# An attention and FFN kernel on one core: the softmax subtracts a row maximum taken by VectorE, and work moves between VectorE, ScalarE and GpSimd

## The chip, the core and the metric

One of the eight cores of a Trainium2 chip runs the whole kernel. The metric is the time of one execution on the device in microseconds (us). Five engines work side by side, each through its own instructions in order: TensorE (PE, matmuls; its weight loads are shown as PEld), VectorE (DVE), ScalarE (ACT), GpSimd (POOL) and SyncE (SP), which here only issues DMAs. They wait for each other through semaphores. PE writes its results to PSUM, eight banks of 128 partitions x 512 fp32 values.

## The reference, cut to what matters

x is 2048 x 448. After a layer norm it goes into an attention (16 query heads of 256, 8 key and value heads, the last 512 positions of the cache) and into a gated FFN; the result is x plus their product.

```
xn = layernorm(x)
q  = xn @ wq                                  # 16 heads of 256
k, v = the last 512 positions of the caches, each for two query heads
p  = softmax(q k^T * 256**-0.5)               # rows of 512
s  = (p v) @ wo
g  = silu((gelu(xn @ w_gate) * (xn @ w_up)) @ w_down)
out = x + s * g
```

Everything is bf16 with fp32 accumulation. A softmax whose rows are shifted by a constant gives the same p, so the kernel before takes the exponentials of the scaled scores as they are, with no maximum subtracted.

## The kernel before

The 2048 rows are cut into four chunks of 512, and each chunk into four tiles of 128. A small recorder (`R.op`) takes each operation with what it reads and writes, derives the semaphore waits from that, and keeps each engine's operations in the order in which the program names them. So the order of the Python loops is the order in each engine's queue.

**Head.** While the first tiles of x are loaded and normalized, PE runs a few warm-up matmuls and folds the last value head with its rows of wo: `fold_tr` (L384) transposes the last head of V into bank 0, `fold_copy` (L393) copies both halves to SBUF in one ACT instruction, `fold` (L397) multiplies them with the last rows of wo ("wo7", loaded by SP between the tiles of x, L301 to L309). The result vw stands in for V and wo of head 15 of every chunk.

**FFN.** For each chunk, 14 pairs of gate and up blocks (`two_blocks`, L464, two matmuls at a time on the two halves of PE's rows), gelu on ACT, product on DVE, then the down projection (`down`, L493). The down projection of the last chunk is spread as filler over the first 21 slots of the attention.

**Attention.** 64 heads follow one another (16 per chunk, index i), each with four tiles t of 128 queries. I call one pass of the inner loop a **slot**; slot n = 4i + t, 256 in all. In a slot (L685 to L703) PE does:

- `scores(i, t)` (L545): two matmuls into bank 4 + n % 2. ACT takes the exponential from PSUM into a bf16 tile `pr` and accumulates the row sum (L556); DVE takes the reciprocal (L558) and multiplies the tile by it (L559); SP transposes it by DMA into `pT` (L562).
- in even slots from slot 12 on, `values` (L564): four matmuls of a head three heads back, into bank 0, 1 or 6 by a list (L570); DVE copies the result to `oT` (L581), ACT for the last two heads.
- in odd slots from head 7 on, half an output projection (`outproj`, L588) of four heads into bank 7; when a tile's second half is done, DVE adds it to `acc` (L627). In the later chunks head 2 has one more in place of the values and head 6 has none (L691 to L701).
- at t = 0 of every eighth head (i = 7, 15, ..., 55), right after that slot's scores and values, the **query burst** (`q_burst`, L516): the queries of the next eight heads, in eight parts. Each part takes a pair of banks, (0,1), (2,3), (4,5) in turn, and is emptied by one ACT copy of 128x1024 (L527); each part's second phase is issued behind the next part's first. The eighth part has banks 2 and 3. A burst of four heads stands in slot 12; its second part has banks 4 and 5.

POOL loads weights during the FFN, and in the attention does SiLU (L646, L648) and the last products (L631, L633), each for one tile of 128 x 448. The score tiles `pr` rotate through 11 buffers.

The order inside a score tile's chain is set by these lines:

```
act(lambda e: e.activation(pr[s][:, :], bank(b), ACT.Exp, scale=scale, accum_out=den[:, s:s + 1]),
    r=[("ps", b)], w=[("pr%d" % s,), ("den", s)])
dve(lambda e: e.reciprocal(rden[:, s:s + 1], den[:, s:s + 1]), r=[("den", s)], w=[("rden", s)])
```

Of the kernel before, what the change touches and what calls it, by code (L numbers as in the profile page):

```python
# [5 lines left out]
ACT = mybir.ActivationFunctionType  # L6
ALU = mybir.AluOpType
BF16 = mybir.dt.bfloat16
F32 = mybir.dt.float32

LN_EPS = 1e-5
P = 128
# [132 lines left out]
def bass_recurrent_scan__sliding_block_cached__geglu_ffn__prompt_kernel(nc, A_x, A_k, A_v, A_wq, A_wo, B_x, B_wg, B_wu, B_wd, out):  # L145
    _, S, D = A_x.shape
    Hkv, Sk, Dh = A_k.shape[1], A_k.shape[2], A_k.shape[3]
    HD = A_wq.shape[1]
    Hq = HD // Dh
    W = min(4096, max(256, Sk // 4))  # L150
    F = B_wg.shape[1]
    QC, TPC, HP, KF = 512, 4, 64, 3
    NQC = S // QC
    NT = NQC * TPC
    NF, NJ, NE = F // P, W // P, Dh // P
    NO = Hq * NE
    assert S % QC == 0 and D == KF * P + HP and NE == 2 and NJ == 4 and Hq == 2 * Hkv and Hq % 4 == 0 and NF % 2 == 0
    scale = float(Dh) ** -0.5
# [3 lines left out]
    with es:  # L162
        off = [16512]

        def sb(name, shape, dt, at=None):
            n = 4 if dt == F32 else 2
            for x in shape[1:]:
                n *= x
            if at is None:
                at = off[0]  # L170
                off[0] += (n + 31) // 32 * 32
            return R.place(name, shape, dt, at), at + (n + 31) // 32 * 32

        ident, _ = sb("ident", [P, P], BF16)
        small, _ = sb("small", [P, 4], F32)
        stats, _ = sb("stats", [P, NT, 6], F32)
        mv, _ = sb("mv", [P, NT, 2], F32)
        std, _ = sb("std", [P, NT], F32)
        rstd, _ = sb("rstd", [P, NT], F32)
        den, _ = sb("den", [P, 16], F32)  # L180
        rden, _ = sb("rden", [P, 16], F32)

        xnT, _ = sb("xnT", [P, NQC, KF + 1, QC], BF16)
        gy, _ = sb("gy", [P, NT, D], BF16)
        kT, _ = sb("kT", [P, Hkv, NE, W], BF16)
        V, _ = sb("V", [P, NJ, Hkv, Dh], BF16)

        wq, _ = sb("wq", [P, KF, Hq, Dh], BF16)
        wq6, _ = sb("wq6", [P, Hq // 2, Dh], BF16)
        wo, _ = sb("wo", [P, Hq * NE, D], BF16)  # L190

        vw, _ = sb("vw", [P, NJ, D], BF16)
# [43 lines left out]
        def bank(b, n=512):  # L236
            return psum[:, b * 512:b * 512 + n]
# [26 lines left out]
        def load_x0(a, b):  # L264
            dma("sync", x4[:, a:b, :], x_view[:, 0, a:b, :], w=[("x4", t) for t in range(a, b)])
# [11 lines left out]
        def load_gu(s):  # L277
            load_w(0, s)
            load_w(1, s)
# [18 lines left out]
        def load_wo7():  # L298
            dma("sync", wo[:, NO - NE:NO, :], wo_v[:, NO - NE:NO, :], w=[("wo", "f")])
# [1 line left out]
        for t in range(2):  # L301
            load_x0(t, t + 1)
        load_v7()
        for t in range(2, TPC):
            load_x0(t, t + 1)
        load_wo7()
        load_gu(0)
        load_gu(1)
        load_gu6(5, NF, "sync")  # L309
# [72 lines left out]
        vT_keys = [("actT", NF - 3), ("actT", NF - 2)]  # L382

        def fold_tr():  # L384
            def run(e):
                for m in range(NE):
                    for j in range(NJ):
                        ins = e.transpose(bank(0).bitcast(BF16)[:, m * W + j * P:m * W + (j + 1) * P],  # L388
                                          V[:, j, Hkv - 1, m * P:(m + 1) * P], ident[:, :])
                return ins  # L390
            pe(run, r=[("V", "f"), ("ident",)], w=[("ps", 0)])

        def fold_copy():  # L393
            act(lambda e: e.activation(vT.rearrange("p m k -> p (m k)"), bank(0).bitcast(BF16), ACT.Copy),  # L394
                r=[("ps", 0)], w=vT_keys)

        def fold(j):  # L397
            def run(e):
# [117 lines left out]
        def q_burst(i0, heads):  # L516

            c, h0 = divmod(i0, Hq)

            def part(n, ph):  # L520
                hp, e_ = divmod(n, 2)
                s, h = 2 * (n % 3 if heads == 8 else (0, 2, 1, 0)[n] if i0 else (n + 2) % 4), h0 + 2 * hp
                buf, name, _ = q_slot(i0 + 2 * hp)
                two_blocks(ph, c, s, [wq[:, :, h + m, e_ * P:(e_ + 1) * P] for m in range(2)],
                           wq6[:, h // 2, e_ * P:(e_ + 1) * P], wq_keys)
                if ph:
                    act(lambda e: e.activation(  # L527
                        buf[:, :, e_, :], psum[:, s * 512:(s + 2) * 512].rearrange("p (a q) -> p a q", a=2), ACT.Copy),
                        r=[("ps", s), ("ps", s + 1)], w=[(name, e_)])

            for n in range(heads + 1):
                if n < heads:
                    part(n, 0)
                if n:
                    part(n - 1, 1)
# [4 lines left out]
        def p_slot(i):  # L540

            n = (i - i // Hq) % NPT
            return (pTf, ("pT", "f")) if folded(i) else (pT[:, n, :, :], ("pT", n))

        def scores(i, t):  # L545
            g, n = (i % Hq) // 2, i * TPC + t
            b, s = 4 + n % 2, n % NPR
            buf, name, a = q_slot(i)

            def run(e):  # L550
                for k in range(NE):
                    ins = e.matmul(bank(b), lhsT=buf[:, a, k, t * P:(t + 1) * P], rhs=kT[:, g, k, :],  # L552
                                   start=k == 0, stop=k == NE - 1)
                return ins
            pe(run, r=[("kT", g), (name, 0), (name, 1)], w=[("ps", b)])
            act(lambda e: e.activation(pr[s][:, :], bank(b), ACT.Exp, scale=scale, accum_out=den[:, s:s + 1]),  # L556
                r=[("ps", b)], w=[("pr%d" % s,), ("den", s)])
            dve(lambda e: e.reciprocal(rden[:, s:s + 1], den[:, s:s + 1]), r=[("den", s)], w=[("rden", s)])  # L558
            dve(lambda e: e.tensor_scalar(pr[s][:, :], pr[s][:, :], rden[:, s:s + 1], None, op0=ALU.mult),  # L559
                r=[("pr%d" % s,), ("rden", s)], w=[("pr%d" % s,)])  # L560
            dst, key = p_slot(i)
            dmaT(dst[:, :, t * P:(t + 1) * P], pr[s][:, :], r=[("pr%d" % s,)], w=[(*key, t)], lane="p%d" % s)  # L562

        def values(i, e_):  # L564
            g = (i % Hq) // 2
            idx = (i % 4) * NE + e_
            src, pkey = p_slot(i)
            at = 2 * i + e_ + 6

            b = (0, 6, 0, 6, 0, 1, 6, 6)[at % 8] if at < 2 * NI else (0, 6, 1, 0, 6, 1)[at - 2 * NI]  # L570

            def run(e):
                for j in range(NJ):
                    ins = e.matmul(bank(b), lhsT=V[:, j, g, e_ * P:(e_ + 1) * P], rhs=src[:, j, :],  # L574
                                   start=j == 0, stop=j == NJ - 1)
                return ins
            pe(run, r=[(*pkey, t) for t in range(TPC)] + ([("V", j) for j in range(NJ)] if g < Hkv - 1 else [("V", "f")]),
               w=[("ps", b)])
            dst, key = oT[(i // 4) % 2][:, idx, :], ("oT%d" % ((i // 4) % 2), idx)
            if i < NI - 2:  # L580
                dve(lambda e: e.tensor_copy(dst, bank(b)), r=[("ps", b)], w=[key])  # L581
            else:
                act(lambda e: e.activation(dst, bank(b), ACT.Copy), r=[("ps", b)], w=[key])

        def n_pieces(G):
            return 3 * NE + NJ if folded(4 * G + 3) else 4 * NE
# [55 lines left out]
        def silu(n):  # L642

            s = n % 2
            act(lambda e: e.activation(tmp[:, s, :], gy[:, n, :], ACT.Tanh, scale=0.5), r=[("gy", n)], w=[("tmp", s)])  # L645
            pool(lambda e: e.tensor_scalar(tmp[:, s, :], tmp[:, s, :], 1.0, 0.5, op0=ALU.add, op1=ALU.mult),  # L646
                 r=[("tmp", s)], w=[("tmp", s)])
            pool(lambda e: e.tensor_tensor(gy[:, n, :], tmp[:, s, :], gy[:, n, :], ALU.mult),  # L648
                 r=[("tmp", s), ("gy", n)], w=[("gy", n)])
# [34 lines left out]
        outs = [(G, t) for G in range(NG) for t in range(TPC)]  # L684
        for i in range(NI):  # L685
            for t in range(TPC):
                scores(i, t)
                if 4 * i + t in fill:
                    down(NQC - 1, *fill[4 * i + t])

                early = i >= Hq and i % Hq == 2  # L691
                if t % 2 == 0 and early:
                    n = n_pieces(outs[1][0])
                    outproj(*outs[1], range(n * t // 4, n * (t + 2) // 4), b=6)
                elif t % 2 == 0 and 4 * i + t >= 12:
                    values(*pv.pop(0))
                if 7 <= i and t % 2 and not (i >= Hq and i % Hq == 6):
                    n = n_pieces(outs[0][0])
                    outproj(*outs[0], range(n * (t - 1) // 4, n * (t + 1) // 4))
                    if t == TPC - 1:  # L700
                        del outs[0:1 + early]  # L701
                if t == 0 and (i == 3 or i % 8 == 7) and i + 1 < NI:
                    q_burst(i + 1, 4 if i == 3 else 8)  # L703
            if i % Hq in (7, 9, 11, 13):
                silu(i // Hq * TPC + (i % Hq - 7) // 2)

        for what in "vvovovo":
            if what == "v":
# [38 lines left out]
```

## Time and profile before

| | us |
|---|---|
| median of 3 runs (lowest, highest) | 558.71 (557.78, 558.84) |
| the profiled execution | 558.57 |
| its span, first to last instruction | 556.8 |
| mean granted TensorE clock | 1.00 |

The span is one profiled execution; what lies around it is 558.57 - 556.8 = 1.8 us. In the span, the head takes the first 10.4 us, the FFN of the four chunks ends at about 127.4 us, the first query burst (four heads) runs from there to 133.6, the slots of the attention run from 133.6 to about 539, and DVE's last product ends at 554.8.

How to read the lines of the profile: L552 is a line of the kernel; then the engine, the operation, output <- input by the program's names (`ps` is PSUM), partitions x elements and type. A line of the timeline begins with the start and the duration in us and ends, in brackets, with the idle time before it and what ended that. Lines with xN are N instructions of one kind with little between them, taken together. SPq rows are DMA issues, with no bracket. ACT's exponential has a second row, ACTIVATION_READ_ACCUMULATOR, which writes out the row sum.

### The profile page before, as it was taken

The numbers are of one execution on the slowest core, as the hardware profiler recorded it, in microseconds if no ns is written. First come the engines' busy times: TensorE is split into PE (matmuls) and PEld (weight loads), VectorE is DVE, ScalarE is ACT, GpSimd is POOL, SyncE is SP. The second block draws the span as 40 slices with busy tenths as digits, with TensorE's granted clock in tenths as the row PEclk, the third lists the DMA queues.
The fourth block names the chain that finished last, engine by engine and source line by source line (L and its number), as shares of the span: only waits on it lengthen the run. The fifth ranks groups of instructions, "written<-read, shape, count | busy, mean of one in ns | idle before, by whom it ended". The sixth has DMA issues, their size and how long they took to land.

```text
span 556.8 us, 9924 instructions
## 1 busy us (share of the span) xinstructions
PE 552.5 (99%) x3550; PEld 261.4 (47%) x3550; DVE 313.7 (56%) x822; ACT 295.6 (53%) x688; POOL 88.4 (16%) x125
## 2 busy tenths in 40 slices
PE   8999999999999999999999999999999999999997
PEld 6444444444444444444444444444444444444445
DVE  5535436043463678077728744772688077628775
ACT  5333324237655665555575556556665655575640
POOL 0131213200000121002301110131121002311134
DMA  8863534952544354245544552547345254635452
GB/s 233 292 140 70 132 86 95 233 146 54 98 86 77 58 98 93 58 85 94 129 75 96 101 95 39 96 95 143 66 96 101 42 86 97 130 79 105 95 96 52
DMA packets 165440, 57.65 MB, mean 104 GB/s; under 512 B 155648, under 2 KB 162304, under 8 KB 165392
## 3 DMA queue, kind: packets, MB, share of 16 engines
q1 hardware_dynamic: 162048, 44.64, 41.5%
q0 software_dynamic: 3040, 12.16, 8.0%
q8 instruction: 28, 0.46, 0.4%
q10 hardware_dynamic: 304, 0.22, 0.1%
q14 instruction: 20, 0.16, 0.1%
HBM read 17.92 MB, written 1.84 MB: 35 GB/s over the span
## 4 chain that ended last, share of the span: by engine, by line
PE 98%; DMA 1%; ACT 0%; SPq 0%; DVE 0%; issue 0%
PE ps L472 33%; PE ps L552 20%; PE ps L574 19%; PE ps L604 18%; PE ps L496 8%; DMA V<-in_A_v_cache_dram 1%; PE ps L400 0%; PE ps L388 0%; ACT actT L394 0%; SPq L249 0%; ACT xnT L370 0%; PE ps L357 0%; ACT std L373 0%; DVE tmp L615 0%; DVE xr L617 0%
## 5 line engine op out<-in xcount | busy, mean ns | idle before, releaser
L556 ACT ACTIVATE pr<-ps 128x512 bf16<-128x512 f32 x256 | 152.5, 597 | 120.4 <-PE ps L552 119.1
L552 PE MATMUL ps<-kT,qT 128*128 128x512 bf16 x512 | 150.9, 380 | 0.0
L558 DVE RECIPROCAL rden<-den 128x1 f32<-128x1 f32 x256 | 41.4, 162 | 154.2 <-ACT pr L556 139.6
L574 PE MATMUL ps<-pT,V 128*128 128x512 bf16 x480 | 123.1, 379 | 0.0
L559 DVE TENSOR_SCALAR pr<-pr,rden 128x512 bf16<-128x512 bf16 x256 | 106.0, 414 | 9.0
L604 PE MATMUL ps<-wo,oT 128*128 128x448 bf16 (+1 forms) x498 | 111.0, 346 | 0.0
L472 PE MATMUL ps<-xnT,wq 64*128 64x512 bf16 x896 | 98.3, 377 | 0.0
L527 ACT ACTIVATE qT<-ps 128x1024 bf16<-128x1024 f32 x64 | 64.5, 1022 | 43.4 <-PE ps L472 43.1
L472 PE MATMUL ps<-xnT,wu 64*128 64x512 bf16 x336 | 82.4, 377 | 0.0
L472 PE MATMUL ps<-xnT,wg 64*128 64x512 bf16 x336 | 82.0, 377 | 0.0
L581 DVE CAST oT<-ps 128x512 bf16<-128x512 f32 x118 | 80.5, 683 | 0.7 <-PE ps L574 0.6
L490 DVE TENSOR_TENSOR actT<-ps,hb 128x512 bf16<-128x512 f32 x56 | 38.5, 692 | 65.9 <-ACT hb L489 61.7
L552 PEld LDWEIGHTS ps<-kT,qT 128*128 128x128 bf16 x512 | 49.2, 98 | 55.4 <-issue 4.0
L574 PEld LDWEIGHTS ps<-pT,V 128*128 128x128 bf16 x480 | 47.0, 98 | 56.3
L604 PEld LDWEIGHTS ps<-wo,oT 128*128 128x128 bf16 x498 | 48.4, 98 | 48.6 <-DVE acc L627 1.0
L472 PEld LDWEIGHTS ps<-xnT,wq 64*128 64x128 bf16 x896 | 43.1, 94 | 54.5 <-DVE rden L558 1.7
L489 ACT ACTIVATE hb<-ps 128x512 bf16<-128x512 f32 x56 | 33.1, 593 | 38.8 <-PE ps L472 38.6
L556 ACT ACTIVATION_READ_ACCUMULATOR pr<-ps 128x1 f32 x256 | 50.2, 196 | 0.0
L496 PE MATMUL ps<-wd,actT 128*128 128x448 bf16 x224 | 46.2, 353 | 0.0
L472 PEld LDWEIGHTS ps<-xnT,wg 64*128 64x128 bf16 x336 | 31.3, 94 | 20.5 <-issue 1.1
L472 PEld LDWEIGHTS ps<-xnT,wu 64*128 64x128 bf16 x336 | 31.3, 94 | 19.9
L646 POOL TENSOR_SCALAR tmp<-tmp 128x448 f32<-128x448 f32 x16 | 9.0, 563 | 197.9 <-ACT tmp L645 197.9
(60 smaller groups left out, 264.0 us busy)
## 6 DMA issues: line engine op xcount, KB each, us to landing
pT<-pr SPq DMA_TRANSPOSE x240, 2.5
wq<-in_A_wq_dram POOLq DMA_DIRECT2D x14, 256.0 KB, 3.6
wo<-in_A_wo_dram POOLq DMA_DIRECT2D x3, 896.0 KB, 9.0
V<-in_A_v_cache_dram POOLq DMA_DIRECT2D x4, 448.0 KB, 6.5
xr<-in_A_x_dram POOLq DMA_DIRECT2D x4, 448.0 KB, 4.2
wd<-in_B_w_down_dram SPq DMA_DIRECT2D x1, 1568.0 KB, 15.1
x<-in_A_x_dram SPq DMA_DIRECT2D x3, 448.0 KB, 9.3
out_dram<-xr POOLq DMA_DIRECT2D x3, 448.0 KB, 3.7
```

The lines of the kernel that those rows point to most:

```text
L472: ins = e.matmul(bank(s + m)[:, q0:q1], lhsT=lhsT, rhs=xnT[lo:lo + HP, c, k, q0:q1], start=ph == 0 and k == 0, stop=ph == 1 and k == KF - 1)
L489: act(lambda e: e.activation(hb[:, h, :], bank(s), ACT.Gelu_apprx_tanh), r=[("ps", s)], w=[("hb", h)])
L490: dve(lambda e: e.tensor_tensor(actT[:, f, :], bank(s + 1), hb[:, h, :], ALU.mult), r=[("ps", s + 1), ("hb", h)], w=[("actT", f)])
L496: pe(lambda e, f=f: e.matmul(bank(b, D), lhsT=actT[:, f, t * P:(t + 1) * P], rhs=wd[:, f, :], start=f == 0, stop=f == NF - 1), r=[("actT", ...
L527: act(lambda e: e.activation(buf[:, :, e_, :], psum[:, s * 512:(s + 2) * 512].rearrange("p (a q) -> p a q", a=2), ACT.Copy), r=[("ps", s), ...
L552: ins = e.matmul(bank(b), lhsT=buf[:, a, k, t * P:(t + 1) * P], rhs=kT[:, g, k, :], start=k == 0, stop=k == NE - 1)
L556: act(lambda e: e.activation(pr[s][:, :], bank(b), ACT.Exp, scale=scale, accum_out=den[:, s:s + 1]), r=[("ps", b)], w=[("pr%d" % s,), ("de ...
L558: dve(lambda e: e.reciprocal(rden[:, s:s + 1], den[:, s:s + 1]), r=[("den", s)], w=[("rden", s)])
L559: dve(lambda e: e.tensor_scalar(pr[s][:, :], pr[s][:, :], rden[:, s:s + 1], None, op0=ALU.mult), r=[("pr%d" % s,), ("rden", s)], w=[("pr%d ...
L574: ins = e.matmul(bank(b), lhsT=V[:, j, g, e_ * P:(e_ + 1) * P], rhs=src[:, j, :], start=j == 0, stop=j == NJ - 1)
L581: dve(lambda e: e.tensor_copy(dst, bank(b)), r=[("ps", b)], w=[key])
L604: ins = e.matmul(bank(b, D)[:, lo:hi], lhsT=lhsT, rhs=rhs, start=idx == 0, stop=idx == n8 - 1)
```

## The change

In words: the scale of the scores moves into the copy of the queries. DVE takes the negated maximum of each score row from PSUM into `nmax`, and the exponential gets it as its bias. Reciprocal, multiply and transposing DMA become a step of their own, `normalize`, which is issued two slots later (`LAG`); the multiply of tile t = 3 goes to POOL. Scores rotate over banks 4, 5, 2 for the first 24 slots and over banks 2 to 5 from then on. All copies of values to `oT` are done by ACT. In the head, wo7 is loaded ahead of x's fourth tile, and the fold's transposes and its copy are split over banks 0 and 1.

```
-        for t in range(2, TPC):
-            load_x0(t, t + 1)
+        load_x0(2, 3)
         load_wo7()
+        load_x0(3, 4)
...
         def fold_tr():
-            def run(e):
-                for m in range(NE):
-                    for j in range(NJ):
-                        ins = e.transpose(bank(0).bitcast(BF16)[:, m * W + j * P:m * W + (j + 1) * P],
-                                          V[:, j, Hkv - 1, m * P:(m + 1) * P], ident[:, :])
+            def run(e, m):
+                for j in range(NJ):
+                    ins = e.transpose(bank(m).bitcast(BF16)[:, j * P:(j + 1) * P], V[:, j, Hkv - 1, m * P:(m + 1) * P], ident[:, :])
                 return ins
-            pe(run, r=[("V", "f"), ("ident",)], w=[("ps", 0)])
+            for m in range(NE):
+                pe(lambda e, m=m: run(e, m), r=[("V", "f"), ("ident",)], w=[("ps", m)])
         def fold_copy():
-            act(lambda e: e.activation(vT.rearrange("p m k -> p (m k)"), bank(0).bitcast(BF16), ACT.Copy),
-                r=[("ps", 0)], w=vT_keys)
+            for m in range(NE):
+                act(lambda e, m=m: e.activation(vT[:, m, :], bank(m).bitcast(BF16)[:, 0:W], ACT.Copy),
+                    r=[("ps", m)], w=[vT_keys[m]])
...
-                        buf[:, :, e_, :], psum[:, s * 512:(s + 2) * 512].rearrange("p (a q) -> p a q", a=2), ACT.Copy),
+                        buf[:, :, e_, :], psum[:, s * 512:(s + 2) * 512].rearrange("p (a q) -> p a q", a=2), ACT.Copy, scale=scale),
...
+        LAG = 2
+        BY_POOL = (3,)
+
+        def s_bank(n):
+            return (4, 5, 2)[n % 3] if n < 6 * TPC else 2 + n % 4
+
         def scores(i, t):
             g, n = (i % Hq) // 2, i * TPC + t
-            b, s = 4 + n % 2, n % NPR
+            b, s = s_bank(n), n % NPR
...
-            act(lambda e: e.activation(pr[s][:, :], bank(b), ACT.Exp, scale=scale, accum_out=den[:, s:s + 1]),
-                r=[("ps", b)], w=[("pr%d" % s,), ("den", s)])
+            dve(lambda e: e.tensor_reduce(nmax[:, s:s + 1], bank(b), mybir.AxisListType.X, ALU.max, negate=True),
+                r=[("ps", b)], w=[("nmax", s)])
+            act(lambda e: e.activation(pr[s][:, :], bank(b), ACT.Exp, bias=nmax[:, s:s + 1], accum_out=den[:, s:s + 1]),
+                r=[("ps", b), ("nmax", s)], w=[("pr%d" % s,), ("den", s)])
+
+        def normalize(i, t):
+            s = (i * TPC + t) % NPR
             dve(lambda e: e.reciprocal(rden[:, s:s + 1], den[:, s:s + 1]), r=[("den", s)], w=[("rden", s)])
-            dve(lambda e: e.tensor_scalar(pr[s][:, :], pr[s][:, :], rden[:, s:s + 1], None, op0=ALU.mult),
-                r=[("pr%d" % s,), ("rden", s)], w=[("pr%d" % s,)])
+            if t in BY_POOL:
+                pool(lambda e: e.tensor_tensor(pr[s][:, :], pr[s][:, :], rden[:, s:s + 1].to_broadcast([P, W]), ALU.mult),
+                     r=[("pr%d" % s,), ("rden", s)], w=[("pr%d" % s,)])
+            else:
+                dve(lambda e: e.tensor_scalar(pr[s][:, :], pr[s][:, :], rden[:, s:s + 1], None, op0=ALU.mult),
+                    r=[("pr%d" % s,), ("rden", s)], w=[("pr%d" % s,)])
             dst, key = p_slot(i)
             dmaT(dst[:, :, t * P:(t + 1) * P], pr[s][:, :], r=[("pr%d" % s,)], w=[(*key, t)], lane="p%d" % s)
...
-            if i < NI - 2:
-                dve(lambda e: e.tensor_copy(dst, bank(b)), r=[("ps", b)], w=[key])
-            else:
-                act(lambda e: e.activation(dst, bank(b), ACT.Copy), r=[("ps", b)], w=[key])
+            act(lambda e: e.activation(dst, bank(b), ACT.Copy), r=[("ps", b)], w=[key])
...
             for t in range(TPC):
+                n = i * TPC + t
                 scores(i, t)
+                if n >= LAG:
+                    normalize(*divmod(n - LAG, TPC))
...
+        for n in range(NI * TPC - LAG, NI * TPC):
+            normalize(*divmod(n, TPC))
```

## The prediction

> **What bounds the kernel now.** First the page: busy time, then the chain that ended last.
>
> ```profile
> PE 552.5 (99%) x3550; PEld 261.4 (47%) x3550; DVE 313.7 (56%) x822; ACT 295.6 (53%) x688; POOL 88.4 (16%) x125
> ...
> PE 98%; DMA 1%; ACT 0%; SPq 0%; DVE 0%; issue 0%
> ```
>
> TensorE (PE) is the bound; nothing else holds 2% of the chain. In the list of waits PE's own come to 1.4 us, all before 10.39 us, where the matmul stream begins. The built order of instructions shows that the change leaves PE's sequence as it is, matmul for matmul. So nothing is to be had behind 10.39 us: there the change can only make PE wait. I therefore looked at what follows each PE write to a bank that now has a new reader. A slot is one score tile (128 queries of one head, 256 slots). The timeline around the query burst at slot 60:
>
> ```profile
> 219.07 0.60 PE L552 MATMUL ps<-kT,qT 128*128 128x512 bf16 x2
> ...
> 219.70 0.60 ACT L556 ACTIVATE pr<-ps 128x512 bf16<-128x512 f32 x1 [0.50 <-PE ps L552]
> ...
> 221.56 0.59 PE L552 MATMUL ps<-kT,qT 128*128 128x512 bf16 x2
> ...
> 221.99 1.03 PE L574 MATMUL ps<-pT,V 128*128 128x512 bf16 x4
> ...
> 222.94 12.26 PE L472 MATMUL ps<-xnT,wq 64*128 64x512 bf16 x112
> ...
> 233.09 1.02 ACT L527 ACTIVATE qT<-ps 128x1024 bf16<-128x1024 f32 x1 [0.49 <-PE ps L472]
> 234.60 1.94 ACT L527 ACTIVATE qT<-ps 128x1024 bf16<-128x1024 f32 x2 [0.49 <-PE ps L472]
> 235.14 0.61 PE L552 MATMUL ps<-kT,qT 128*128 128x512 bf16 x2
> 235.58 0.92 PE L604 MATMUL ps<-wo,oT 128*128 128x448 bf16 x4
> 236.34 0.60 PE L552 MATMUL ps<-kT,qT 128*128 128x512 bf16 x2
> ```
>
> Matmuls overlap, so I count from start to start: scores 0.43 us, values 0.86, half an output projection 0.76. An even slot is 1.30, an odd one 1.19, four are 4.98. A score is ready for its reader 0.63 after its start (219.07 to 219.70). The burst follows slot 60 directly, and the scores of slot 61 (235.14) follow the burst directly, while ScalarE's (ACT's) last two query copies run until 234.60 + 1.94 = 236.54. Before, slot 61 writes bank 5, freed long ago; the last copy reads banks 2 and 3.
>
> VectorE (DVE), three rows of its timeline beside GpSimd's (POOL's):
>
> ```profile
> 198.05 1.03 POOL L648 TENSOR_TENSOR gy<-tmp,gy 128x448 bf16<-128x448 f32 x1
> 198.07 0.16 DVE L558 RECIPROCAL rden<-den 128x1 f32<-128x1 f32 x1
> 198.27 0.96 DVE L559 TENSOR_SCALAR pr<-pr,rden 128x512 bf16<-128x512 bf16 x1
> ...
> 199.16 0.68 DVE L581 CAST oT<-ps 128x512 bf16<-128x512 f32 x1
> 199.76 0.15 DVE L558 RECIPROCAL rden<-den 128x1 f32<-128x1 f32 x1
> 199.94 0.35 DVE L559 TENSOR_SCALAR pr<-pr,rden 128x512 bf16<-128x512 bf16 x1
> ```
>
> A multiply (L559) takes 0.35 alone and 0.96 where POOL's tensor_tensor runs: it ends with POOL's, and the next DVE instruction starts 0.08 behind it. The reciprocal is not held. DVE's instructions overlap too: reciprocal to multiply 0.20, multiply to the next 0.27 (201.02 - 200.76 = 0.26 elsewhere), CAST to the next 0.60 for a duration of 0.68.
>
> **The change, step by step.**
>
> Row maximum: 256 reductions, 128x512 from PSUM; before has none. Nearest row, L581 (same shape read from PSUM): 0.68 long, 0.60 to the next. Bounds: 0.53 to the next (three of L409's 448 columns take 1.68, one 0.61) and 0.68. I take 0.60, and 0.68 until the exponential may start. The 118 CASTs go to ACT (0.60 each, L583), a quarter of the multiplies to POOL: L633's 1.03 for 448 columns, by width 1.18. Bounds 1.0 and, should the broadcast operand be slow, 2.1, twice L633's.
>
> Exponential: a bias by pointer. The square root with one takes 292 ns (L373), the same width without 203 (L291): +0.09, 0.69 in all; bounds 0.60 and 0.69. ACT then has, per four slots, 4 x (0.69 + 0.10) + 2 x 0.60 = 4.4 of 4.98: no bound by itself. The scale moved into the query copy costs nothing (an immediate either way).
>
> DVE per four slots: 4 maxima 2.40, 3 x (0.20 + 0.27) = 1.41, a reciprocal 0.10, one accumulation 0.55: 4.46 of 4.98. Each slot queues its maximum, then the reciprocal and multiply of the slot two before; the accumulation stands behind t=3. Followed in that order with t=0 at time 0: the t=0 maximum stands behind the accumulation of the slot before and starts at 1.06 instead of 0.63; maxima t=1, 2, 3 start at 2.13, 3.12, 4.42; POOL's multiply runs 2.97 to 4.15 and costs the one multiply behind it about 0.2. The next t=0 starts at 1.06 again: DVE just keeps up. With 0.68 for a maximum it is 1.14. So:
>
> 1. **Behind a burst.** Slot 61 now takes bank 2 + 61 % 4 = 3, which the last query copy reads: PE waits from 235.14 to 236.54, 1.40 us. Every 8-head burst ends so (behind slot 28 the last two copies start at 182.57 and run 1.94, and PE goes on at 183.11: again 1.40): 7 x 1.40 = **9.8**. Bounds 1.2 to 1.9 each.
> 2. **Into a burst.** The second part writes banks 2 and 3, 2.16 us after the burst slot starts; bank 2 holds that slot's scores. Maximum from 1.06, exponential from 1.79, done 2.48, seen 2.53: PE waits 0.37, say 0.4; 7 x 0.4 = **2.8**. Bounds 0 (DVE free at 0.63) and 1.0.
> 3. **Slots 4 to 12.** Here PE needs only 0.76 a slot (137.95 to 144.05 for eight), there are three banks, and DVE needs 1.07 with a multiply, 0.70 without, plus up to 0.6 per POOL multiply. Maximum 4 starts at 139.1 behind the down-projection's CAST; with 1.07, 0.70 and POOL's locks the ninth starts at 144.4, its exponential is done 1.47 later, 145.84, and only then may scores 12 (144.05 before) write that bank: 1.8 late. Maximum 12 starts at 148.05 behind another CAST, its exponential ends at 149.5, and the second part of the 4-head burst, which writes bank 4 too, would be there at 148.0: 1.5 more. **3.3**; bounds 2 and 5.
> 4. **Slots 21 to 28.** No projection yet, 0.87 a slot. Slot 24 takes bank 2 right after slot 23 (the new rule of banks): maximum 23 starts at 166.6, its exponential ends at 168.07, slot 24 was due at 166.07: 2.0. The burst behind slot 28 then waits 0.9 instead of the 0.4 of step 2: **2.5** in all; bounds 1 and 3.5.
> 5. **Heads 22, 38, 54** have no projection: four slots in 3.46 for a DVE that needs 4.2, and a burst follows: 3 x 0.8 = **2.4**; bounds 1 and 4.
> 6. **Two values in bank 6 running**, two slots apart. The copy is now on ACT behind the t=0 exponential and ends 0.2 too late; eight such pairs between bursts: **1.6**; bounds 0 and 4.
> 7. **POOL's other work** (16 SiLU pairs, 32 products) holds multiplies while DVE has little to spare: in the trace 28 of 256 multiplies take 0.75 or more. Bounds 0 and 8; I take **2**, nearer to the rows in which DVE has slack.
> 8. **Head.** The fold matmuls start at 7.78, when wo7 lands (issued 3.13, 4.5 to landing). Issued 0.5 earlier, they start when the warm-up matmuls end, 7.55: **-0.2**. The split copy ends 0.4 earlier, hidden by that DMA. x's fourth tile, 0.5 later, still makes its transpose at 9.34. Bounds -0.5 and +0.3.
>
> Hidden: SP has one transposing DMA per slot as before, in the same order, now behind POOL's multiply every fourth time; values use a tile 7 slots (8.7 us) after its normalization is issued, and multiply plus landing is 1.2 + 2.5. At the end PE has 14 us of work behind the last scores, so the lag of two shows nowhere.
>
> Sum: 9.8 + 2.8 + 3.3 + 2.5 + 2.4 + 1.6 + 2.0 - 0.2 = 24.2. The profiled execution took 558.57 (span 556.8), 0.14 under the median: 558.57 + 24.2 = **582.8**.
>
> **Rivals.**
>
> A. *DVE becomes the bound* between bursts, if its instructions don't overlap: 4 x 0.68 + 4 x 0.16 + 3 x 0.35 + 0.62 + a lock of 0.44 = 5.47 for 4.98. Over 56 heads 27 us, with steps 1 and 3 558.57 + 27.4 + 9.8 + 3.3 = 599. For it: DVE has under 0.5 us to spare per head. Against: the spacings above. The Trainium skill ("VectorE: DVE Perf Modes", The DRAIN you can't avoid) says the next instruction doesn't start until the pipe is empty, save where it isn't held; the 0.60 behind a 0.68 CAST is the exception, so the rule itself would give this rival, the rows do not.
>
> B. *Only the fixed wait remains*: DVE keeps up everywhere but in slots 4 to 12 (lower bound 2): 558.57 + 9.8 + 2 = 570.4. For it: DVE is 56% busy. Against: slots at 0.76 us.
>
> C. *PE's clock drops after the waits.* The first 32 matmuls of 128 columns take 3.60 us, 0.11 each; eight of the same later 0.62, at most 0.08: PE starts slow for some 3.6 us. If each burst's wait brought that back, 1.8 us lost each: 582.8 + 12.6 = 595. Against: the granted clock reads 1.00 everywhere, and 1.4 us is short. The Trainium skill ("TensorE: Matmul & The Clock Gate", A second HAM failure mode) reports a clock that swings from small idles between banks; no row here shows it.
>
> D. *Not slower*: the head's earlier start of 0.2 (at most 0.5) is all that is left, 558.3. It decides if the last query copy is out before slot 61 starts; it would have to end 1.40 earlier, with ACT free before it and PE's last part still to come. Faster by more than 0.5 has no place.
>
> **How the numbers follow.** Forecast (574 to 592) 0.62; A 0.15; B 0.14; C 0.05; D 0.04. The range takes in A, B and C: 570 to 600. About 0.2% (1.1 us) is what a measurement here can tell: slower 0.96, same 0.02, faster 0.02.
>
> **What will show it.** Step 1: seven waits of PE at the score line for ACT's query copy, 1.4 each. Steps 2 to 5: PE waits at the query line and at scores for ACT's exponential, near 138 to 170 us and ahead of the bursts. Step 6: values waiting for ACT's copy. The maximum's row: 0.68. POOL's multiply: 1.2. A is right if PE waits in every head; B if only step 1 is there. I am wrong in kind if PE has no wait at the score line behind a burst.

## The result, and the profile after

The changed kernel takes **584.37 us** (median of 4 runs, 583.20 to 584.89) against 558.78 before: the ratio is 1.0459, 95% interval 1.0446 to 1.0473. The forecast was 582.8. The profiled execution has a span of 583.1 us, 26.3 longer. Its page opens with the busy times; further down stand the groups of the new work (mean ns of one, then the idle time before them and its releaser):

```profile
PE 554.1 (95%) x3517; PEld 264.2 (45%) x3550; DVE 356.6 (61%) x896; ACT 375.2 (64%) x807; POOL 154.2 (26%) x189
...
L563 DVE TENSOR_REDUCE nmax<-ps 128x1 f32<-128x512 f32 x256 | 175.5, 686 | 138.6 <-PE ps L559 134.1
L565 ACT ACTIVATE pr<-ps,nmax 128x512 bf16<-128x512 f32 x256 | 175.9, 687 | 77.2 <-PE ps L590 29.8
...
L572 POOL TENSOR_TENSOR pr<-pr,rden 128x512 bf16<-128x512 bf16 x64 | 66.6, 1041 | 237.0 <-DVE rden L570 233.2
...
L575 DVE TENSOR_SCALAR pr<-pr,rden 128x512 bf16<-128x512 bf16 x192 | 75.8, 395 | 6.8
```

PE's busy time grew by 1.6 us, its span by 26.3: PE waits. (Of PE's 3550 matmuls 33 have no record in this trace; all weight loads have.) Neither DVE nor ACT comes near its limit on the whole. The page's chain breaks off after a tenth of the span, as it does in some traces with all records, so PE's own waits are the view to read (total us, times, longest):

```profile
PE ps L559 <- ACT qT L528: 11.3, 7, 1.6
PE ps L473 <- ACT pr L565: 4.7, 8, 1.1
PE ps L559 <- ACT pr L565: 2.9, 4, 2.0
PE ps L590 <- ACT oT L596: 2.2, 7, 0.6
PE ps L590 <- DMA pT<-pr: 1.6, 1, 1.6
```

The first line is the wait behind the bursts: scores (L559) for the query copy (L528), seven times. Its 11.3 us is too high, because all seven times the first matmul behind the wait is one without a record. The second is the wait into the bursts (L473 for the exponential), the third slots 4 to 12 and slot 24, the fourth the values in bank 6. The fifth was not forecast. The burst of slot 60, in the changed kernel's timeline:

```profile
230.79 0.59 PE L559 MATMUL ps<-kT,qT 128*128 128x512 bf16 x2
...
231.22 1.03 PE L590 MATMUL ps<-pT,V 128*128 128x512 bf16 x4
231.30 0.62 DVE L640 TENSOR_TENSOR acc<-ps,acc 128x448 f32<-128x448 f32 x1
...
231.83 0.68 DVE L563 TENSOR_REDUCE nmax<-ps 128x1 f32<-128x512 f32 x1
232.18 1.04 PE L473 MATMUL ps<-xnT,wq 64*128 64x512 bf16 x8
...
232.60 0.69 ACT L565 ACTIVATE pr<-ps,nmax 128x512 bf16<-128x512 f32 x1 [0.81 <-PE ps L590]
...
233.18 0.19 ACT L565 ACTIVATION_READ_ACCUMULATOR pr<-ps,nmax 128x1 f32 x1
...
233.52 11.40 PE L473 MATMUL ps<-xnT,wq 64*128 64x512 bf16 x104 [0.30 <-ACT pr L565]
...
244.31 1.94 ACT L528 ACTIVATE qT<-ps 128x1024 bf16<-128x1024 f32 x2 [0.49 <-PE ps L473]
246.30 0.11 PEld L559 LDWEIGHTS ps<-kT,qT 128*128 128x128 bf16 x2 [1.88 <-ACT qT L528]
246.53 0.38 PE L559 MATMUL ps<-kT,qT 128*128 128x512 bf16 x1 [1.61 <-ACT qT L528]
```

The maximum of slot 60 starts 1.04 us after its scores (forecast 1.06), behind the accumulation at 231.30. The burst's second part waits for that slot's bank. Behind the burst the weight loads of the scores start 0.05 after the last copy's end, 246.25. The row at 246.53 is the second of the two matmuls (x1 where there should be x2).

Because PE's instructions are the same in both kernels, the start of each weight load can be set against the same one in before. The difference grows where PE waits or its clock falls, and only there. That gives the whole loss by place:

| place | forecast, us | in the trace |
|---|---|---|
| 1 behind seven bursts | 9.8 | 10.2 (7 x 1.46) |
| 2 into seven bursts | 2.8 | 3.3 (7 x 0.47) |
| 3 slots 4 to 12 | 3.3 | 3.1 |
| 4 slot 24 and the burst behind it | 2.5 | 2.5 |
| 5 heads without projection | 2.4 | 1.2 (3 x 0.40) |
| 6 values in bank 6 | 1.6 | 2.8 (8 pairs) |
| 7 GpSimd's other work | 2.0 | no place of its own |
| 8 head | -0.2 | -0.2 |
| PE's clock behind slot 24 | rival C | 1.7 |
| last values | 0 | 1.8 |
| sum (from unrounded terms) | 24.2 | 26.3 |

Step 8's -0.2 can't be told from chance. The start of the matmul stream differs by more than that from run to run: over the eleven traces with the changed head it lies from 0.69 us earlier to 0.83 us later than in the one trace of before, and in two of the variants below that keep before's head 0.16 earlier and 0.14 later.

### The profile page after: what moved, and what is told of

The parts are those of the page before. It is cut to its first block, busy times and chain, and to the rows that moved or that the text cites. A ratio compares the mean times of both kernels' runs of the same rounds, so it can differ in the third digit from the quotient of the medians.

```text
span 583.1 us, 10429 instructions
## 1 busy us (share of the span) xinstructions
PE 554.1 (95%) x3517; PEld 264.2 (45%) x3550; DVE 356.6 (61%) x896; ACT 375.2 (64%) x807; POOL 154.2 (26%) x189
## 5 line engine op out<-in xcount | busy, mean ns | idle before, releaser
L563 DVE TENSOR_REDUCE nmax<-ps 128x1 f32<-128x512 f32 x256 | 175.5, 686 | 138.6 <-PE ps L559 134.1
L565 ACT ACTIVATE pr<-ps,nmax 128x512 bf16<-128x512 f32 x256 | 175.9, 687 | 77.2 <-PE ps L590 29.8
L559 PE MATMUL ps<-kT,qT 128*128 128x512 bf16 x487 | 146.3, 381 | 15.5 <-ACT qT L528 11.3
L572 POOL TENSOR_TENSOR pr<-pr,rden 128x512 bf16<-128x512 bf16 x64 | 66.6, 1041 | 237.0 <-DVE rden L570 233.2
L473 PE MATMUL ps<-xnT,wq 64*128 64x512 bf16 x896 | 99.7, 376 | 4.7 <-ACT pr L565 4.7
L528 ACT ACTIVATE qT<-ps 128x1024 bf16<-128x1024 f32 x64 | 64.6, 1023 | 33.5 <-PE ps L473 33.2
L473 PE MATMUL ps<-xnT,wu 64*128 64x512 bf16 x336 | 82.3, 376 | 0.0
L473 PE MATMUL ps<-xnT,wg 64*128 64x512 bf16 x336 | 82.0, 376 | 0.0
L559 PEld LDWEIGHTS ps<-kT,qT 128*128 128x128 bf16 x512 | 49.0, 98 | 70.6 <-ACT qT L528 13.1
L575 DVE TENSOR_SCALAR pr<-pr,rden 128x512 bf16<-128x512 bf16 x192 | 75.8, 395 | 6.8
L596 ACT ACTIVATE oT<-ps 128x512 bf16<-128x512 f32 x120 | 70.6, 589 | 6.0 <-PE ps L590 5.8
L473 PEld LDWEIGHTS ps<-xnT,wq 64*128 64x128 bf16 x896 | 47.2, 94 | 56.5 <-DVE pr L575 5.7
L565 ACT ACTIVATION_READ_ACCUMULATOR pr<-ps,nmax 128x1 f32 x256 | 50.1, 196 | 0.0
L473 PEld LDWEIGHTS ps<-xnT,wg 64*128 64x128 bf16 x336 | 31.3, 94 | 20.5 <-issue 1.1
L473 PEld LDWEIGHTS ps<-xnT,wu 64*128 64x128 bf16 x336 | 31.3, 94 | 19.9
```

The source lines that it names most:

```text
L473: ins = e.matmul(bank(s + m)[:, q0:q1], lhsT=lhsT, rhs=xnT[lo:lo + HP, c, k, q0:q1], start=ph == 0 and k == 0, stop=ph == 1 and k == KF - 1)
L528: act(lambda e: e.activation(buf[:, :, e_, :], psum[:, s * 512:(s + 2) * 512].rearrange("p (a q) -> p a q", a=2), ACT.Copy, scale=scale), ...
L563: dve(lambda e: e.tensor_reduce(nmax[:, s:s + 1], bank(b), mybir.AxisListType.X, ALU.max, negate=True), r=[("ps", b)], w=[("nmax", s)])
L565: act(lambda e: e.activation(pr[s][:, :], bank(b), ACT.Exp, bias=nmax[:, s:s + 1], accum_out=den[:, s:s + 1]), r=[("ps", b), ("nmax", s)], ...
L572: pool(lambda e: e.tensor_tensor(pr[s][:, :], pr[s][:, :], rden[:, s:s + 1].to_broadcast([P, W]), ALU.mult), r=[("pr%d" % s,), ("rden", s) ...
```

## The experiments

My theory: PE loses time only where a PSUM bank changes hands too late, at the places above. The main rival: VectorE is the bound between bursts, so a wait mended in one place comes back in another. Unless said otherwise a number is the median of 4 runs, against 558.2 to 558.6 for before, run beside it.

**Burst banks rotated.**

```
-                s, h = 2 * (n % 3 if heads == 8 ...
+                s, h = 2 * ((n + 2) % 3 if heads == 8 ...
```

> The changed kernel, with the banks of the 8-head bursts rotated by one pair, (4,5), (0,1), (2,3), so that the last part has banks 0 and 1 and the second part no longer has the bank of the scores just issued. Theory (PE waits only where a PSUM bank changes hands): the waits behind the bursts (7 x 1.45 = 10.2 us) and those into the bursts (4.5 us) go and nothing takes their place: 584.4 - 14.7 = 569.7. Rival (VectorE is the bound between bursts, and these waits only let it catch up): the time comes back as other waits, 578 or more.

Measured 571.55, ratio 1.0238 (1.0221 to 1.0255). The line of scores waiting for the query copy is gone:

```profile
PE ps L559 <- ACT pr L565: 2.6, 3, 2.0
PE ps L473 <- DVE nmax L563: 2.1, 3, 0.7
PE ps L473 <- ACT pr L565: 1.5, 2, 1.1
PE ps L590 <- DMA pT<-pr: 1.3, 1, 1.3
PE ps L590 <- ACT oT L596: 1.2, 4, 0.3
```

12.8 us came back for one changed expression, with no work taken away. Of the 14.7 expected, 0.78 each by the weight loads stayed ahead of the bursts behind heads 22, 38 and 54 (the second line) and 0.4 at slot 28: the first part now has the banks of the last scores of a head in which DVE is late. The second line names the maximum, but what PE waits for is the exponential of the last scores: at slot 92 the accumulator row of slot 91's exponential ends at 283.05 and the weight loads go on at 283.16, the same 0.11 as at the burst of slot 60 in the changed kernel.

**Score banks shifted by one.**

```
-            return (4, 5, 2)[n % 3] if n < 6 * TPC else 2 + n % 4
+            return (4, 5, 2)[n % 3] if n < 6 * TPC else 2 + (n + 1) % 4
```

> The changed kernel, with the score banks from slot 24 on shifted by one (2 + (n + 1) % 4): the slot behind a burst takes bank 4, and slot 24 takes bank 3 instead of slot 23's bank 2. The slot of the burst takes bank 3, which the burst's second part writes too. Theory: the waits behind the bursts (10.2) and at slot 24 (2.1, and the 1.6 us that PE ran at half clock behind it) go, those into the bursts stay: 584.4 - 13.9 = 570.5, some 1 us more if VectorE comes later to slot 28. Rival (VectorE is the bound): 578 or more. If the clock falls for another reason than the wait at slot 24, it falls here too.

Measured 571.71, 1.0244 (1.0229 to 1.0260). The waits of step 1 and at slot 24 are gone by another edit than the last one, the waits into the bursts stay (4.8 us in 8 waits), and so does the one at the end (1.9). The clock never falls while PE has work. At slot 28 the wait is 0.75 us longer than in the changed kernel, as the expectation allowed.

**No maximum**: the 256 reductions and the bias are left out, so rows are exponentiated unshifted, as in before.

```
-            dve(lambda e: e.tensor_reduce(nmax[:, s:s + 1], bank(b), ...))
-            act(lambda e: e.activation(pr[s][:, :], bank(b), ACT.Exp, bias=nmax[:, s:s + 1], ...))
+            act(lambda e: e.activation(pr[s][:, :], bank(b), ACT.Exp, ...))
```

> The changed kernel without the 256 row maxima and the bias of the exponential; banks, lag, GpSimd's multiplies and ScalarE's copies stay as changed. Theory: the waits behind the bursts don't depend on the maximum and stay (10.2), with up to 2 us at the end of the kernel; the rest (slots 4 to 12, slot 24, into the bursts, bank 6) goes: 558.6 + 10.2 + 1 = 570. Rival (the maximum's load on VectorE is the cause of all): 558 to 560.

Measured 570.41, 1.0221 (1.0206 to 1.0237):

```profile
PE ps L559 <- ACT qT L528: 9.7, 7, 1.4
...
PE ps L559 <- ACT pr L563: 0.9, 1, 0.9
PE ps L588 <- DMA pT<-pr: 0.7, 1, 0.7
```

This is the run that parts the two theories most clearly: with the maximum gone, 10.2 us by the weight loads remain behind the bursts. They belong to the choice of banks. The 0.9 is slot 24, where the same bank is used twice running. The maximum itself is worth 14.0 us (584.37 - 570.41), at the other places and in the clock.

**No GpSimd**: `BY_POOL = ()`.

> The changed kernel with all multiplies on VectorE, none on GpSimd. Theory: VectorE has 4.46 + 0.37 = 4.83 us of work for 4.98 in four slots and no locks from these multiplies, so all stays within 1.5 us: 583 to 586. Rival 1 (GpSimd's lock on VectorE's multiply is a large part of the loss): under 580. Rival 2 (VectorE needs the relief): over 590.

Measured 584.42, 1.0472 (1.0456 to 1.0488): no change. In its trace 0.46 more is lost ahead of each of the bursts behind heads 22, 38 and 54 and 0.7 more up to slot 28, 0.6 less at the last values, and the fall of the clock (1.7) did not happen in this run. The two runs of the changed kernel whose mean clock (1.000 and 0.999) leaves no room for such a fall took 583.20 and 584.21, these four 583.84 to 584.84. So at equal clock GpSimd's multiplies, with their lock, are worth under 1 us; what the lock alone costs no run shows. Some rows bear on the lock, from the changed kernel:

```profile
228.94 0.69 DVE L563 TENSOR_REDUCE nmax<-ps 128x1 f32<-128x512 f32 x1 [0.19 <-PE ps L559]
229.02 1.04 POOL L572 TENSOR_TENSOR pr<-pr,rden 128x512 bf16<-128x512 bf16 x1
...
229.74 0.47 DVE L575 TENSOR_SCALAR pr<-pr,rden 128x512 bf16<-128x512 bf16 x1
```

The maximum runs its usual 0.69 beside GpSimd's multiply, while the multiply on DVE is held (0.47 instead of 0.35) until shortly after that one ends, 230.21 against 230.06. The Trainium skill ("SBUF — State Buffer", Who interferes with whom) says that a reduction never contends with GpSimd and that a two-port tensor_scalar is blocked for the whole instruction; both agree with these rows.

**Copies of the values on VectorE**, as before the change.

```
+            if i < NI - 2:
+                dve(lambda e: e.tensor_copy(dst, bank(b)), ...)
+            else:
                 act(lambda e: e.activation(dst, bank(b), ACT.Copy), ...)
```

> The changed kernel with the copies of the values on VectorE again, as before the change. Theory: VectorE then has 4.46 + 1.2 = 5.66 us of work for four slots of 4.98, is the bound between bursts, and PE waits at scores in every head: 56 x 0.7 = 39 us, some of it in place of waits that are there already: 610 to 625. Rival (VectorE, 61% busy, has room): 583 to 587.

Measured 627.91, 1.1238 (1.1214 to 1.1263): 43.5 us more than the changed kernel, a little over the 26 to 41 expected; the clock fell three times in its trace, not once, which at 1.7 each would be some 3 us of it. This is what rival A looks like when it is real. PE's waits now name DVE and come in most heads (two lines of them), and between bursts DVE's queue has stretches without gaps (each start follows the one before by the spacing of that instruction):

```profile
PE ps L620 <- DVE acc L643: 11.2, 23, 0.7
...
PE ps L620 <- DVE acc L641: 7.8, 12, 0.7
```

```profile
232.49 0.68 DVE L597 CAST oT<-ps 128x512 bf16<-128x512 f32 x1
233.09 0.68 DVE L563 TENSOR_REDUCE nmax<-ps 128x1 f32<-128x512 f32 x1
233.69 0.15 DVE L570 RECIPROCAL rden<-den 128x1 f32<-128x1 f32 x1
233.87 0.35 DVE L575 TENSOR_SCALAR pr<-pr,rden 128x512 bf16<-128x512 bf16 x1
234.14 0.62 DVE L643 TENSOR_TENSOR acc<-ps,acc 128x448 f32<-128x448 f32 x1
234.67 0.68 DVE L563 TENSOR_REDUCE nmax<-ps 128x1 f32<-128x512 f32 x1
```

CAST, maximum, accumulation: 0.60, 0.60, 0.53 from start to start. In the changed kernel 4.46 us of such spacings fit into 4.98; with 1.2 more they don't.

**The maximum alone**, put into the kernel before, with its two banks and no lag (2 runs).

```
+            dve(lambda e: e.tensor_reduce(nmax[:, s:s + 1], bank(b), ..., ALU.max, negate=True), ...)
-            act(lambda e: e.activation(pr[s][:, :], bank(b), ACT.Exp, scale=scale, ...))
+            act(lambda e: e.activation(pr[s][:, :], bank(b), ACT.Exp, bias=nmax[:, s:s + 1], ...))
```

> The kernel before with the row maximum alone: maximum on VectorE, bias in the exponential, scale in the query copy; two score banks, no lag, all multiplies and copies on VectorE as before. Theory: VectorE then goes through maximum, wait for the exponential and its sum, reciprocal, multiply in each slot: 0.68 + 0.05 + 0.77 + 0.05 + 0.20 + 0.27 = 2.0, and 0.44 for copies and accumulations, 2.46 for slots of 1.245; 256 slots, with the bursts beside only two of each 32: 790 to 820. Rival (the waits overlap and only the instructions count, 0.68 + 0.47 + 0.44 = 1.6): 640 to 660.

Measured 859.12, 1.5386 (1.5355 to 1.5417). The chain through maximum, exponential, reciprocal and multiply sets most slots (PE waits 172.9 us for the exponential in 207 places). The price of a slot was right: outside the bursts and at full clock a slot takes 2.44 us in the mean, 2.46 expected. 256 x (2.44 - 1.245) is about 305 us, near the 300 measured over before, so the 40 to 70 us by which the expectation is short are mostly what it took off for the bursts. The granted clock stands at 0.5 for 86 us of this run, which explains little: slots of tile t = 2 wholly at half clock took 2.64 us, at full clock 2.45. Together the lag, the banks and the moved copies and multiplies are worth 275 us to a kernel that wants the maximum; no run parts the lag from the banks.

**Normalizations issued ahead of the bursts.**

```
+                burst = t == 0 and (i == 3 or i % 8 == 7) and i + 1 < NI
+                while todo and (todo[0] <= n - LAG or burst and todo[0] <= n):
+                    normalize(*divmod(todo.pop(0), TPC))
```

> The changed kernel, with the normalizations that are still due issued ahead of each query burst, so that the lag of two is not carried past it. Theory (SyncE issues one transposing DMA in 1.3 us and the slots come at 1.245; the two transposes that the lag pushes behind the last burst make the last values late): the wait of the values at the end, 1.8 us, goes: 584.4 - 1.8 = 582.6. Rival (GpSimd's products hold up the last tiles): 584.4, the wait stays.

Measured 583.71, 1.0442 (1.0413 to 1.0471). The wait at the end is still there, 2.0 us by the weight loads: that part of my theory is wrong (the reason is given below, with SP's queue). The 0.7 us by which the total is shorter is no more than the clock, which did not fall in this trace.

**A lag of one slot**: `LAG = 1`.

> The changed kernel with a lag of one slot instead of two. Theory (the last values wait for transposes whose tiles come two slots later than before, behind a SyncE queue that runs 3.5 us late in both kernels): the wait of the values at the end falls from 1.8 by one slot, 1.25, to about 0.5, all else stays: 583.1. Rival (the end waits for something else): 584.4 with 1.6 or more at the end.

Measured 584.82, 1.0484 (1.0465 to 1.0503). The wait at the end fell from 1.8 to 1.3, by less than half of the slot that the tiles come earlier; 0.45 each came up ahead of three bursts, and 0.5 up to slot 28. The clock did not fall in this trace.

**Four hand-overs mended**: rotated burst banks, shifted score banks, normalizations ahead of the bursts, and

```
-            b = (0, 6, 0, 6, 0, 1, 6, 6)[at % 8] ...
+            b = (0, 6, 0, 6, 0, 1, 6, 1)[at % 8] ...
```

> The changed kernel with four of its hand-overs mended together: burst banks rotated, score banks shifted by one, normalizations issued ahead of the burst, and bank 1 instead of the second bank 6 for values. All work of the changed kernel is still there. Theory: 584.4 - 10.2 (behind bursts) - 4.5 (into bursts) - 3.7 (slot 24 and the clock behind it) - 2.8 (bank 6) - 1.8 (end) = 561.4, plus 1.7 that stayed ahead of bursts with rotated banks: 563; of the loss there remain slots 4 to 12, 3.1. Rival (VectorE is short of time, and waits mended in one place come up in another): 570 or more.

Measured 567.63, 1.0160 (1.0141 to 1.0179): 16.7 us of the 25.6 are back, against 21 expected. Waits into the bursts, at slot 24 and in bank 6 are gone. But 7 x 0.54 are new: rotated *and* shifted, slot 29 has bank 4, which the burst's seventh part has just used. I made that hand-over myself. Of what is left over before, these are 3.8 us, slots 4 to 12 3.1 and the end 2.0.

**Mended again**: as above, but score banks 3, 4, 5, 2 in slots 24 to 27 and 3, 2, 4, 5 from slot 28, the lag one, and normalizations not moved ahead.

> The changed kernel with rotated burst banks, bank 1 instead of the second bank 6 for values, score banks 3, 4, 5, 2 in slots 24 to 27 and 3, 2, 4, 5 in turn from slot 28, so that no slot behind a burst meets the last two parts' banks, and a lag of one instead of two. All work of the changed kernel is still there. Theory: against the kernel with the four mends (567.6) the 7 x 0.54 behind the bursts go, 3.8, and of the 2.1 at the end some 1.3: 562.5, with slots 4 to 12 (3.1) as the largest rest. Rival (with so little lag VectorE waits for the exponential, or its shortage of time shows in another place): 567 or more.

Measured 567.77, 1.0178 (1.0149 to 1.0207), the same. The 7 x 0.54 are gone, and in their place stand 3 x 1.2 ahead of the bursts behind heads 22, 38 and 54 (the rotated first part meets bank 5's late scores; 0.45 of each comes from the lag of one, as in the run with that alone) and 2.1 at the end. The rival has the number and a part of the reason: in these heads DVE has more work than time (step 5), and its lateness comes out at the next bank that PE wants. The wait at the end is of another kind.

**The head alone**, in the kernel before (10 runs).

> The kernel before with the head of the changed one alone (wo7 ahead of x's fourth tile, fold transposes and copies in two banks). Theory: the matmul stream starts 0.2 us earlier and nothing else moves: 558.3, within 0.2% of before, the shift visible in the trace alone. Rival (x's fourth tile comes too late for its transpose): the stream starts up to 0.3 us later.

Measured 558.43, 0.9999 (0.9990 to 1.0008): no change that can be measured. In the trace the stream starts 0.15 us earlier, no more than it differs between runs of one head. None of the versions is measurably faster than the kernel before.

**Waits of chosen length**, in the kernel before: at twelve slots PE waits for 1 to 12 extra copies on ACT.

```
+            for _ in range(DELAY.get(n, 0)):
+                held = [act(lambda e: e.activation(pause[:, :], wo[:, 0, 0:256], ACT.Copy), ...)]
-            pe(run, ...)
+            pe(run, ..., after=held)
```

> The kernel before, in which PE is made to wait at twelve slots for 1 to 12 extra copies of 128x256 on ScalarE (some 0.45 us each, nothing reads their result), to see which wait lowers PE's granted clock. Theory: a wait of about 2 us or more lowers it to 0.5 for some 3.4 us, one under 1.5 does not. Rival (the fall at slot 24 has to do with PSUM banks or was chance): no wait under 5 us lowers it.

One run, 610.36. The first four waits (1.1 to 1.8 us) leave the granted clock at 1.00; the other eight (2.9 to 5.4) each lower it to 0.50 for 3.41 or 6.83 us.

## Why the prediction was right, point by point

The kind, most places and the sum were right: the bound stays PE, nothing is gained behind 10.39 us, and PE loses at bank hand-overs. Two places, the clock and the last values, were put at nothing, and step 7 forecast a loss that isn't there.

- **Step 1** was right in mechanism and nearly in size: 1.46 for 1.40. The rest is the 0.05 from the end of ACT's copy to PE's next weight load.
- **Steps 2, 3, 4** were right (0.47 for 0.40; 3.1 for 3.3; 2.5). The prices under them held: the maximum 0.686 long and 0.60 to the next, the exponential 0.687. In step 2 PE goes on 0.23 after the exponential's own end; I had taken 0.05. In the trace it is the row that reads the accumulator, and not the exponential's, that updates the semaphore PE waits for, and PE's weight loads follow that row's end by 0.11.
- **Step 5** was mis-sized, 0.40 for 0.8 a head.
- **Step 6** had the eight pairs and 0.2 for four of them; the other four cost 0.45 to 0.5, three of these behind a head with one more projection. 2.8 for 1.6.
- **Step 7** failed: GpSimd's SiLU and products make no wait of their own. They do hold multiplies (the multiplies on DVE take 395 ns in the mean and up to 1157, where the median is 354), but at no place where PE waits. GpSimd's multiply took 1.04, not 1.18.
- **Step 8** forecast a gain of 0.2, which these runs can't tell from the scatter of the head.
- **"At the end PE has 14 us of work behind the last scores, so the lag of two shows nowhere"** failed: 1.8. I had called SP's queue hidden because its number of DMAs is unchanged, and had not read its pace. The timeline of SP in the changed kernel, and then in before:

```profile
557.20 9.07 SPq L253 DMA_TRANSPOSE pT<-pr  x7
566.36 5.15 SPq L253 DMA_TRANSPOSE pTf<-pr  x4
```

```profile
518.94 20.26 SPq L252 DMA_TRANSPOSE pT<-pr  x15
539.29 5.14 SPq L252 DMA_TRANSPOSE pTf<-pr  x4
```

SP issues one transpose in 1.31 us ((566.36 - 557.20) / 7), slots come at 1.245. So SP falls behind after each burst, by 3.4 us at slot 251 in before and 3.6 in the changed kernel (from the end of the multiply to the issue), and only the next burst lets it catch up. Behind the last burst there is none. From the start of the scores behind the last burst (slot 221) to the issue of slot 251's transpose it is 42.6 us in before and 46.6 in the changed kernel. Of these 4.0 us, 2.6 are the two transposes that the lag pushes behind the burst, and 1.4 are longer pauses between two issues (2.09 and 2.48 us at the longest, 2.02 in before). Why SP pauses there stays open. PE itself comes 0.7 later to these values, and in before they had 1.3 to spare: 4.0 - 0.7 - 1.3 is the 2.0 us by which their first weight load is late, of which PE makes up 0.2.

The other runs fit. In nine traces these values wait 0.9 us or more. In eight of them their weight loads start 2.6 to 2.7 us after the issue of slot 251's transpose (such a transpose takes 2.5 to landing); in the run without the maximum it is 3.4. Moving the two transposes ahead of the burst took them out of that stretch, but the first one behind the burst was then issued 4.4 us after slot 221's start instead of 2.7, and SP then waited longer for tiles that were not ready yet; so nothing was gained. That SP's pace is the cause at the end follows from these rows; no run made SP's queue shorter to show it.

- **Rival A** was not what happened, and the run with the copies on VectorE shows that it was near: 1.2 us more in four slots and it is the bound. **Rival B** undershot, since steps 2 to 6 are there. **Rival C** happened once, not behind a burst but behind the longest wait, and not in every run.

The sum came to 24.2 for 26.3, but errors of both signs met in it: 3.4 too much in steps 3, 5 and 7, 5.6 too little in steps 1, 2 and 6, the clock and the end. So 22.8 of the 26.3 us stand at forecast places and for the reasons given there; that the sum came within some 2 us is in part luck.

## What to carry to other kernels

When a change hands PSUM banks to a new use, list for each bank who touched it last and when that reader ends: one wrong pair in a rotation cost 1.46 us seven times here, and changing an index gave 12.8 us back, nearly the 14.0 that leaving out the maximum gave. An engine's load per stretch says whether it can keep up (4.46 in 4.98 did, 5.66 did not); what it costs on the way is decided by the few places where its lateness meets a bank that PE wants. Read the pace of every queue, those that only issue DMAs too: 1.31 against 1.245 is hidden only as long as something lets it catch up.

## What the runs showed of the hardware that was not expected

PE's granted clock is decided in stretches of 3.41 us. In every trace that has records of the clock, the times at which it changed lie whole multiples of 3.41 apart (in the changed kernel 167.25, 3.41 and 409.60 us, which is 49, 1 and 120 times 3.413), from a start that differs from run to run. The stretch around slot 24's wait and the two behind it, from the changed kernel (start and end, length, PE busy; PEclk is the third number from the end):

```profile
167.84:171.25 3.41, 1.44 (x8) 0.52 (x6) 2.72 (x8) 2.71 (x7) 1.04 (x1) 1.00 0.38 73
171.25:174.66 3.41, 3.41 (x9) 1.18 (x8) 1.12 (x4) 1.38 (x3) 0.00 (x0) 0.50 0.44 84
174.66:178.07 3.41, 3.41 (x18) 1.39 (x18) 3.34 (x9) 2.57 (x7) 1.04 (x1) 1.00 0.25 48
```

Behind 1.44 us of work in a stretch the next one ran at half clock: nine matmuls instead of eighteen. The stretches with a burst's wait in them have 1.80 us of work or more in the changed kernel, and the clock stayed full behind each. The wait at slot 24 in the run with the normalizations moved ahead fell across the border of two stretches, 2.16 and 2.70 us busy, and cost nothing more:

```profile
166.93:170.34 3.41, 2.16 (x10) 0.78 (x8) 3.03 (x9) 2.73 (x8) 1.04 (x1) 1.00 0.40 77
170.34:173.75 3.41, 2.70 (x13) 1.29 (x14) 2.10 (x7) 1.88 (x5) 0.00 (x0) 1.00 0.56 108
```

Taken over all stretches of all traces in which the clock was full, half clock always followed 1.30 us of work or less (12 times), and never 1.71 or more. In between, from 1.40 to 1.70, it followed 17 times and did not 11 times, most of them in the run with the maximum alone. With a lag of one the clock stayed full behind 1.42, with shifted banks behind 1.55, and with rotated banks it fell behind 1.45. So the work in a stretch isn't all that decides, and what else does stays open. A wait of 2.1 to 2.3 us at slot 24 cost 1.7 us more in two traces and nothing more in three. The Trainium skill ("TensorE: Matmul & The Clock Gate", What's actually happening) has a free-running window of 3413 ns, which agrees; it has the clock fall after an idle window, while here a window with 42% of work was enough.
